# Moving the low-part subtraction of 32 weight pieces from VectorE to GpSimd, with a new order of work

## The chip, the cores and the metric

The program runs on one core of a Trainium2 chip. The metric is device time in microseconds (us): 932.86 us is the median of three runs (932.21 to 934.22). The engines have short names: PE (TensorE), DVE (VectorE), ACT (ScalarE), POOL (GpSimd) and SP (SyncE, which issues the loads here). A change of under 0.2% (1.9 us) can't be told from none with this kernel.

## What is computed

Two steps, all in fp32. Attention over 8 batches, 8 heads, 576 positions of 64 numbers, where each position sees only a few others (a band of 32 for four heads, every 32nd position for the other four); and a feed-forward layer on the 4608 tokens that come out:

```python
attn = softmax(mask(q @ k.T / 8)); x = (attn @ v)          # x: 4608 x 512
h  = x @ w_in                                              # 512 -> 2048
sp = np.maximum(h, 0.0) + np.log1p(np.exp(-np.abs(h)))
g  = h * erf(sp)
out = g @ w_out                                            # 2048 -> 512
```

The weights arrive as 64-bit floats.

## The kernel before

**Split numbers.** A product that is to be exact to fp32 is taken as three products of reduced precision. Each operand is split into a high part (a cast on ACT) and a low part (the number less its high part, on DVE). This is done for x (`xhi`, `xlo`), for g (`ghi`, `glo`) and for the weights (`pair[:, 0]`, `pair[:, 1]`).

**Weight pieces.** `weight()` prepares one of 32 pieces (pieces 0 to 15 of w_in, 16 to 31 of w_out), each 128x512. SP loads the 64-bit words; three DVE operations (`bits0`, `bits1`, `bits2`, L628 to L641) make an fp32 number in `w`; ACT casts it to the high part (L646); a fourth DVE operation, `split_lo_w` (L649), subtracts to get the low part.

**Attention units.** `heads()` does one batch and one pair of heads (called b0 hp3 for batch 0, pair 3): scores on PE (L400, masks L413), softmax on DVE and ACT (maximum L436, exponentials L457 or L472, sums, reciprocal L490 and L491), the multiplication by the reciprocal on POOL (L498, for most units), transposes on PE (L507) with a copy by ACT (L513), and the product with v on PE (L526), whose result is split into `xhi` and `xlo` (L545, L550). The eight units of batches 0 and 1 come first; later ones are strewn into the feed-forward work.

**Feature tiles.** `ftile()` handles 384 tokens and 128 of the 2048 features: 12 matmuls of the first product (L678, tile `h`), ten steps of activation on ACT (L686, L716) and DVE (L683, L713, L719) that end in `ghi` and `glo`, and 9 matmuls of the second product (L750, tiles `o`). There are 192 of these. `h` has three buffers, so a tile's first product waits until the `glo` of the tile three before it is done. "First product 5" below is that of the fifth tile.

**Order.** Nothing is scheduled by hand. Every operation has an engine, a duration by formula and a sort key; `Plan.order()` walks through time and lets each engine take the ready operation with the smallest key. The keys are the tables `FT`, `KW` and `KP`. The list that comes out is emitted in that order, so each engine runs its list strictly in order. Three rules of the planner matter below. `TWO` and `op.locks` make some DVE operations and every POOL operation exclude one another. `BLOCK = 254` counts PE's instructions, with a pause possible at each 254th while the next instructions are brought in. And `warm()` puts matmuls without use into PE's gaps.

Of the kernel before, what the change touches and what calls it, by code (L numbers as in the profile page):

```python
# [8 lines left out]
F32 = mybir.dt.float32  # L9
# [4 lines left out]
ALU = mybir.AluOpType  # L14
# [17 lines left out]
FT = (31.6335, -135.614, 224.291, 52.3709, -149.741, 22.9733, 45.4447, 151.185, -55.3448, 2.76331, -71.5147, 15.0393)  # L32
KI = 6.0
KW = (
# [39 lines left out]
PAIRS = (
# [192 lines left out]
def attention_moe(  # L267
# [52 lines left out]
    def act(n, fixed=0.093):  # L320
        return fixed + n / 1200.0
# [643 lines left out]
```

## Time and profile before

| | |
|---|---|
| median of 3 runs | 932.86 us |
| profiled execution | 933.05 us, span 931.3 us |
| PE busy | 909.7 us (98%) |
| DVE busy | 686.7 us (74%), 1352 instructions |
| ACT busy | 653.4 us (70%) |
| POOL busy | 60.9 us (7%), 59 instructions |
| mean granted PE clock | 0.993 of full |

An engine's busy share is a mean over a program with three parts: a head of some 60 us in which attention for the first two batches and the first weights are made ready, a long middle of feature tiles, and a short end. The table by stretches (below) is to be read before the totals. A row of the timeline gives start, duration, engine, line, operation, tiles, and in brackets how long the engine was idle before it and what ended that.

### The profile page before, as it was taken

What the parts mean: (1) busy time and instruction counts of PE and PEld (TensorE: products, weight loads), DVE (VectorE), ACT (ScalarE), POOL (GpSimd) and SP (SyncE); (2) the same over time, 40 slices, a digit from 0 to 9 for tenths busy, and PEclk for the clock granted to TensorE, in tenths of its full rate; (3) what the DMA queues carried; (4) which work ended last, traced back from release to release, by engine and by line L of the source; (5) the groups of instructions that cost most, each with busy time, mean ns of one, the idle gap of its engine ahead of it and who ended that gap; (6) DMA issues with size and microseconds to landing.
All of it is one profiled execution on the core that took longest, in us unless ns stands there. A gap on an engine that the chain in (4) does not pass through costs nothing.

```text
span 931.3 us, 20134 instructions
## 1 busy us (share of the span) xinstructions
PE 909.7 (98%) x8166; PEld 809.6 (87%) x8169; DVE 686.7 (74%) x1352; ACT 653.4 (70%) x1476; POOL 60.9 (7%) x59
## 2 busy tenths in 40 slices
PE   5789999999999999999999999999999999999998
PEld 4678888898888889988888899998898899999997
DVE  5999999996757766669886876667876666666664
ACT  5687887887776767667666666766766766766765
POOL 2200012110101100001110100000100000000000
PEclk9799999999999999999999999999999999999999
DMA  9994124321313010013312300002300200000000
GB/s 336 391 362 154 62 57 73 61 34 48 78 58 86 30 64 35 27 57 105 99 56 92 124 17 1 34 1 73 135 1 30 70 1 1 34 1 0 34 1 35
DMA packets 23421, 68.86 MB, mean 74 GB/s; under 512 B 2592, under 2 KB 3232, under 8 KB 23328
## 3 DMA queue, kind: packets, MB, share of 16 engines
q1 hardware_dynamic: 20736, 62.86, 18.9%
q0 software_dynamic: 2592, 4.72, 3.6%
q8 instruction: 64, 1.05, 0.5%
q14 instruction: 29, 0.24, 0.1%
HBM read 53.41 MB, written 14.16 MB: 73 GB/s over the span
## 4 chain that ended last, share of the span: by engine, by line
PE 90%; DVE 4%; ACT 3%; issue 1%; DMA 1%; SPq 0%; POOL 0%; ACTq 0%; POOLq 0%
PE h L678 41%; PE o L750 40%; PE s L400 3%; PE x L526 3%; PE t L507 2%; PE s L526 1%; DMA qk<-qk_loc 1%; ACT b L686 1%; DVE a L683 1%; DVE b L683 1%; ACT a L686 1%; PE s L507 1%; DVE glo L719 1%; ACT sm L472 0%; DVE h L713 0%
## 5 line engine op out<-in xcount | busy, mean ns | idle before, releaser
L750 PE MATMUL o<-pair,ghi 128*128 128x512 f32 x1152 | 361.4, 395 | 0.2 <-ACT ghi L716 0.2
L678 PE MATMUL h<-xhi,pair 128*128 128x384 f32 x1536 | 302.4, 339 | 0.6 <-DVE glo L719 0.6
L678 PEld LDWEIGHTS h<-xhi,pair 128*128 128x128 f32 x1536 | 271.4, 188 | 16.5 <-DVE glo L719 2.6
L686 ACT ACTIVATE b<-b 128x384 f32<-128x384 f32 x384 | 200.4, 522 | 77.2 <-DVE b L683 73.8
L750 PEld LDWEIGHTS o<-pair,ghi 128*128 128x128 f32 x1152 | 209.8, 188 | 32.4 <-ACT ghi L716 0.7
L750 PE MATMUL o<-pair,glo 128*128 128x512 f32 x576 | 224.8, 390 | 0.0
L683 DVE SCALAR_TENSOR_TENSOR a<-h,a 128x384 f32<-128x384 f32 x192 | 106.3, 553 | 83.3 <-ACT a L686 82.8
L678 PE MATMUL h<-xlo,pair 128*128 128x384 f32 x768 | 164.4, 336 | 0.0
L686 ACT ACTIVATE a<-h 128x384 f32<-128x384 f32 x192 | 93.5, 487 | 100.9 <-PE h L678 100.2
L683 DVE SCALAR_TENSOR_TENSOR a<-a,h 128x384 f32<-128x384 f32 x192 | 105.5, 549 | 68.9 <-ACT b L686 68.9
L713 DVE TENSOR_TENSOR h<-b,h 128x384 f32<-128x384 f32 x192 | 107.0, 557 | 46.2 <-ACT b L686 45.8
L678 PEld LDWEIGHTS h<-xlo,pair 128*128 128x128 f32 x768 | 136.0, 188 | 0.0
L750 PEld LDWEIGHTS o<-pair,glo 128*128 128x128 f32 x576 | 108.1, 188 | 23.7 <-DVE glo L719 0.3
L686 ACT ACTIVATE a<-a 128x384 f32<-128x384 f32 x192 | 100.3, 523 | 26.6 <-DVE a L683 26.1
L719 DVE TENSOR_TENSOR glo<-h,ghi 128x384 fp32r<-128x384 f32 x192 | 105.7, 550 | 11.7 <-ACT ghi L716 10.2
L716 ACT CAST ghi<-h 128x384 fp32r<-128x384 f32 x192 | 90.5, 471 | 29.1 <-DVE h L713 15.1
L683 DVE SCALAR_TENSOR_TENSOR b<-b,a 128x384 f32<-128x384 f32 x192 | 108.7, 566 | 1.0
L686 ACT ACTIVATE b<-a 128x384 f32<-128x384 f32 x192 | 101.0, 526 | 4.4
L498 POOL TENSOR_TENSOR sm<-sm,r 128x768 f32<-128x768 f32 (+3 forms) x36 | 45.0, 1249 | 435.3 <-DVE r L491 330.9
L436 DVE TENSOR_REDUCE mx<-s 128x12 f32<-128x768 f32 (+3 forms) x37 | 28.8, 784 | 10.6 <-PE s L413 10.3
L766 ACT COPY ob<-o 128x512 f32<-128x512 f32 x54 | 31.0, 588 | 2.7 <-PE o L750 2.2
L526 PEld LDWEIGHTS x<-pt,v 64*64 64x64 f32 x1392 | 24.4, 135 | 6.9 <-issue 4.4
(49 smaller groups left out, 511.4 us busy)
## 6 DMA issues: line engine op xcount, KB each, us to landing
out<-ob SPq DMA_DIRECT2D x36, 256.0 KB, 2.0
v<-v_loc SPq DMA_DIRECT2D x13, 640.0 KB, 4.1
words<-w_in SPq DMA_DIRECT2D x16, 512.0 KB, 8.6
words<-w_out SPq DMA_DIRECT2D x16, 512.0 KB, 9.1
qk<-qk_loc SPq DMA_DIRECT2D x13, 592.0 KB, 3.8
qk<-qk_str SPq DMA_DIRECT2D x12, 608.0 KB, 3.8
v<-v_str SPq DMA_DIRECT2D x16, 384.0 KB, 3.3
out<-ob POOLq DMA_DIRECT2D x18, 256.0 KB, 4.6
```

Of the source, the lines that this page charges most:

```text
L436: yield nc.vector.tensor_reduce(out=mx[:, parts[i], :units], in_=wide(of(s, i)), axis=mybir.AxisListType.X, op=ALU.max)
L498: yield (nc.gpsimd if pool_norm else nc.vector).tensor_tensor(out=d, in0=d, in1=spread(rc, i), op=ALU.mult)
L507: yield nc.tensor.transpose(bank(t, h)[:, 128 * w : 128 * w + 128], sm[:, h, c : c + 128], ident)
L526: yield nc.tensor.matmul(bank(px, m)[h * D : (h + 1) * D, a * n : (a + 1) * n], values(rows, (2 * a + h) * D), pt[rows, h, c : c + n], sta ...
L678: yield nc.tensor.matmul(ph[:, :CH], win[4 * s + cc][:, w, fs], x[cc][:, c0 : c0 + CH], start=(i == 0), stop=(i == len(terms) - 1))
L683: yield nc.vector.scalar_tensor_tensor(out=out, in0=in0, scalar=scalar, in1=in1, op0=op0, op1=op1)
L686: yield nc.scalar.activation(dst, src, func, bias=bias[i], scale=scale)
L713: yield nc.vector.tensor_tensor(out=ph[:, :CH], in0=bb.tile, in1=ph[:, :CH], op=ALU.mult)
L716: yield nc.scalar.copy(ghi.tile, ph[:, :CH])
L719: yield nc.vector.tensor_tensor(out=glo.tile, in0=ph[:, :CH], in1=ghi.tile.bitcast(F32), op=ALU.subtract)
L750: yield nc.tensor.matmul(po.tile, g[:, ts], wout[f][:, w], start=(f == first_f and i == 0), stop=(f == last_f and i == 2),)
L766: yield nc.scalar.copy(ob.tile, po.tile)
```

## The change

`split_lo_w` is issued on GpSimd for all 32 pieces. In the planner it gets another duration and the engine `pool`. The tables `FT`, `KW` and `KP` have new numbers throughout, so that the whole program stands in another order.

```diff
-FT = (31.6335, -135.614, 224.291, 52.3709, -149.741, 22.9733, 45.4447, 151.185, -55.3448, 2.76331, -71.5147, 15.0393)
+FT = (22.3696, -56.4987, 194.434, 53.4017, -119.353, -10.553, 57.033, 135.384, -40.4697, 20.41, -109.684, 14.539)
...
+POOL_LO = tuple(range(32))
...
         def split_lo_w():
-            yield nc.vector.tensor_tensor(out=pair[:, 1], in0=w.tile, in1=pair[:, 0].bitcast(F32), op=ALU.subtract)
+            yield (nc.gpsimd if i in POOL_LO else nc.vector).tensor_tensor(
+                out=pair[:, 1], in0=w.tile, in1=pair[:, 0].bitcast(F32), op=ALU.subtract
+            )
...
         op = add("act", act(n), key + 0.3, split_hi, [op], [pair], [w])
+        if i in POOL_LO:
+            return add("pool", 0.1 + n / 500.0, key + 0.4, split_lo_w, [op], [], [w, pair]), pair
         return add("dve", dve(n), key + 0.4, split_lo_w, [op], [], [w, pair]), pair
```

The lines after it move by one to five (L649 becomes L650, L678 becomes L683, L719 becomes L724, L750 becomes L755).

What moves is shown at three places. The first is DVE at its first weight piece (piece 2, `w_2`), before:

```order
L641 SCALAR_TENSOR_TENSOR w_2_190<-words_98,w_2_190 128x512
L481 TENSOR_REDUCE r_2_235<-sm_2_158 128x12
L490 TENSOR_SCALAR r_2_235<-r_2_235 128x12
L491 RECIPROCAL r_2_235<-r_2_235 128x12
L649 TENSOR_TENSOR pair_283<-w_2_190,pair_283 128x512
```

DVE at the same piece now:

```order
L642 SCALAR_TENSOR_TENSOR w_2_156<-words_94,w_2_156 128x512
L465 TENSOR_SCALAR mx_1_159<-mx_1_159 128x5
L437 TENSOR_REDUCE mx_2_253<-s_2_170 128x12
L491 TENSOR_SCALAR r_1_198<-r_1_198 128x5
L492 RECIPROCAL r_1_198<-r_1_198 128x5
```

The subtraction into `pair` is gone from DVE's list; it is the first thing in POOL's list now.

The second place is PE between the first products of tiles 4 and 5 (`h_1076` and `h_1182` before), after the last matmul of tile 4. `s_2_927` is the last attention unit of batch 1, `pair_846` and `pair_997` are weight pieces of w_out. Before:

```order
L507 MATMUL s_2_927<-ident,sm_2_928 128x128 x6
L750 MATMUL o_0_1110<-pair_846,ghi_1037 128x512 x2
L750 MATMUL o_0_1110<-pair_846,glo_1048 128x512
L750 MATMUL o_0_1120<-pair_846,ghi_1037 128x512 x2
L750 MATMUL o_0_1120<-pair_846,glo_1048 128x512
L526 MATMUL s_2_927<-qk_1_2_766,v_2_856 64x54 x22
L750 MATMUL o_0_1158<-pair_846,ghi_1037 128x512 x2
L750 MATMUL o_0_1158<-pair_846,glo_1048 128x512
L750 MATMUL o_0_1110<-pair_997,ghi_1124 128x512 x2
L750 MATMUL o_0_1110<-pair_997,glo_1153 128x512
L750 MATMUL o_0_1120<-pair_997,ghi_1124 128x512 x2
L750 MATMUL o_0_1120<-pair_997,glo_1153 128x512
```

PE in the same place now (`h_1046` and `h_1211` are tiles 4 and 5, `s_0_917` is the last attention unit of batch 1, `s_0_1164` the first of batch 2):

```order
L508 MATMUL s_0_917<-ident,sm_0_918 128x128 x6
L755 MATMUL o_0_1081<-pair_980,ghi_1006 128x512 x2
L755 MATMUL o_0_1081<-pair_980,glo_1036 128x512
L755 MATMUL o_0_1089<-pair_980,ghi_1006 128x512 x2
L755 MATMUL o_0_1089<-pair_980,glo_1036 128x512
L527 MATMUL s_0_917<-qk_1_0_638,v_0_744 64x32 x32
L527 MATMUL s_0_917<-qk_1_0_638,qk_1_0_639 64x32 x4
L755 MATMUL o_0_1144<-pair_980,ghi_1006 128x512 x2
L755 MATMUL o_0_1144<-pair_980,glo_1036 128x512
L401 MATMUL s_0_1164<-qk_0_1033 32x64 x40
L683 MATMUL h_1211<-xhi_76,pair_437 128x384
```

Six matmuls of the second product have gone behind first product 5, and the 40 score matmuls of the first unit of batch 2 have come ahead of it.

The third place is DVE between the `glo` of the first tile (`glo_1048`) and that of the second (`glo_1153`). Before, all that stands there:

```order
L683 SCALAR_TENSOR_TENSOR a_1006<-a_1006,h_962 128x384
L498 TENSOR_TENSOR sm_2_928<-sm_2_928,r_2_1018 128x768
L683 SCALAR_TENSOR_TENSOR b_1033<-b_1033,a_977 128x384
L550 TENSOR_TENSOR xlo_83<-s_1_3_858,xhi_79 128x18x18
L550 TENSOR_TENSOR xlo_83<-s_1_3_859,xhi_79 128x18x14
L683 SCALAR_TENSOR_TENSOR b_1043<-b_1043,a_1006 128x384
L641 SCALAR_TENSOR_TENSOR w_18_959<-words_673,w_18_959 128x512
L713 TENSOR_TENSOR h_898<-b_1033,h_898 128x384
L628 TENSOR_SCALAR w_7_1117<-words_690 128x512
L683 SCALAR_TENSOR_TENSOR a_1108<-h_1076,a_1108 128x384
L635 SCALAR_TENSOR_TENSOR w_7_1117<-words_690,w_7_1117 128x512
L719 TENSOR_TENSOR glo_1153<-h_898,ghi_1124 128x384
```

DVE between the first and second tile's `glo` now has 20 rows (two for a reciprocal, eight of 384 numbers, four of `xlo`, two `bits0`, four `bits1` or `bits2`); the last twelve are:

```order
L688 SCALAR_TENSOR_TENSOR b_1062<-b_1062,a_967 128x384
L642 SCALAR_TENSOR_TENSOR w_9_915<-words_702,w_9_915 128x512
L688 SCALAR_TENSOR_TENSOR a_1079<-h_1046,a_1079 128x384
L629 TENSOR_SCALAR w_19_1095<-words_645 128x512
L629 TENSOR_SCALAR w_20_1137<-words_751 128x512
L636 SCALAR_TENSOR_TENSOR w_19_1095<-words_645,w_19_1095 128x512
L636 SCALAR_TENSOR_TENSOR w_20_1137<-words_751,w_20_1137 128x512
L718 TENSOR_TENSOR h_854<-b_1039,h_854 128x384
L551 TENSOR_TENSOR xlo_80<-s_0_917,xhi_76 128x256
L551 TENSOR_TENSOR xlo_80<-s_0_917,xhi_76 128x320
L718 TENSOR_TENSOR h_885<-b_1062,h_885 128x384
L724 TENSOR_TENSOR glo_1206<-h_854,ghi_1157 128x384
```

Twelve rows have become twenty: two more pieces are begun here, and the last unit's `xlo` stands here as well.

## Rows read from the trace of the kernel before

**Rows 1.** The table by stretches of time: stretch, its length, then busy us (and instructions) of PE, PE's weight loads, DVE, ACT and POOL, the granted PE clock, the share of the DMA engines, GB/s.

```profile
20.00:30.00 10.00, 4.90 (x164) 3.45 (x155) 8.05 (x21) 7.58 (x37) 2.84 (x3) 0.91 1.02 371
30.00:40.00 10.00, 8.12 (x222) 6.54 (x223) 9.60 (x23) 7.10 (x29) 3.53 (x4) 0.67 1.03 403
...
50.00:60.00 10.00, 8.26 (x88) 5.71 (x87) 9.90 (x25) 8.38 (x36) 1.94 (x2) 1.00 1.03 409
60.00:70.00 10.00, 9.33 (x128) 8.17 (x126) 10.00 (x22) 7.58 (x18) 0.00 (x0) 1.00 0.81 297
...
100.00:120.00 20.00, 19.44 (x99) 17.45 (x98) 20.00 (x41) 15.73 (x35) 0.00 (x0) 1.00 0.20 73
...
900.00:931.30 31.30, 27.47 (x134) 23.69 (x132) 15.71 (x31) 18.01 (x39) 0.00 (x0) 1.00 0.07 26
```

**Rows 2.** The timeline of PE in the head, around three idle times that end with "issue".

```profile
22.21 0.44 PE L400 MATMUL s<-qk,qk 64*64 64x64 f32 x10 [1.92 <-issue]
...
24.67 0.88 PE L400 MATMUL s<-qk,qk 64*32 64x64 f32 x67
28.66 0.46 PE L400 MATMUL s<-qk,qk 64*32 64x64 f32 x13 [3.12 <-issue]
...
32.38 0.55 PE L526 MATMUL s<-pt,v 64*64 64x32 f32 x24
34.68 1.47 PE L526 MATMUL s<-pt,v 64*64 64x32 f32 x48 [1.75 <-issue]
```

**Rows 3.** The timeline of PE further on: first product 1, the first useless matmul of the wait for the softmax of b1 hp3, the second half of that unit's product with v, and first product 4.

```profile
43.69 2.37 PE L678 MATMUL h<-xhi,pair 128*128 128x384 f32 x8
...
54.74 0.38 PE L863 MATMUL warm<-con 128*128 128x512 bf16 x1
...
60.74 0.90 PE L526 MATMUL s<-qk,v 64*64 64x54 f32 x42 [0.67 <-ACT qk L513]
61.57 1.68 PE L678 MATMUL h<-xhi,pair 128*128 128x384 f32 x8
```

**Rows 4.** The timeline of ACT for the same softmax: its first and last exponential, and the last copy of its transposes.

```profile
52.24 0.31 ACT L472 ACTIVATE sm<-s,mx 128x64 f32<-128x64 f32 x1
...
55.80 0.39 ACT L472 ACTIVATE sm<-s,mx 128x64 f32<-128x64 f32 x1
...
60.10 0.59 ACT L513 COPY qk<-s 128x384 f32<-128x384 f32 x1
```

**Rows 5.** Groups of instructions by line and shape: count, busy us in all, mean ns of one, idle time before them.

```profile
L649 DVE TENSOR_TENSOR pair<-w,pair 128x512 fp32r<-128x512 f32 x32 | 22.8, 712 | 0.9 <-ACT pair L646 0.9
...
L498 POOL TENSOR_TENSOR sm<-sm,r 128x768 f32<-128x768 f32 x13 | 19.4, 1493 | 90.7 <-DVE r L491 51.8 <-ACT b L686 22.0 <-PE o L750 8.3
...
L448 DVE TENSOR_TENSOR sm<-s,mx 128x640 f32<-128x640 f32 x13 | 10.6, 818 | 0.3
```

**Rows 6.** The timeline of POOL: two of its twelve multiplications in the first 60 us.

```profile
20.11 0.72 POOL L498 TENSOR_TENSOR sm<-sm,r 128x320 f32<-128x320 f32 x1 [2.89 <-DVE r L491]
...
38.14 1.26 POOL L498 TENSOR_TENSOR sm<-sm,r 128x640 f32<-128x640 f32 x1 [0.44 <-ACT qk L513]
```

**Rows 7.** The timeline of DVE: the four operations beside POOL's work that took longer than their like (20.19, 30.62, 34.06 and 38.19), and at 32.90 the like of the second.

```profile
20.19 1.20 DVE L641 SCALAR_TENSOR_TENSOR w<-words,w 128x512 uint32<-128x512 uint32 x1
...
30.62 0.72 DVE L464 TENSOR_SCALAR mx<-mx 128x5 f32<-128x5 f32 x1
...
32.90 0.16 DVE L464 TENSOR_SCALAR mx<-mx 128x5 f32<-128x5 f32 x1
...
34.06 1.26 DVE L628 TENSOR_SCALAR w<-words 128x512 uint32<-128x512 uint32 x2
...
38.19 1.75 DVE L649 TENSOR_TENSOR pair<-w,pair 128x512 fp32r<-128x512 f32 x1
```

**Rows 8.** The timeline of DVE without a gap; from one start to the next is what an operation costs DVE.

```profile
64.19 0.68 DVE L641 SCALAR_TENSOR_TENSOR w<-words,w 128x512 uint32<-128x512 uint32 x1
64.79 0.55 DVE L713 TENSOR_TENSOR h<-b,h 128x384 f32<-128x384 f32 x1
65.25 0.42 DVE L628 TENSOR_SCALAR w<-words 128x512 uint32<-128x512 uint32 x1
65.59 0.55 DVE L683 SCALAR_TENSOR_TENSOR a<-h,a 128x384 f32<-128x384 f32 x1
...
67.12 0.68 DVE L649 TENSOR_TENSOR pair<-w,pair 128x512 fp32r<-128x512 f32 x1
67.72 0.55 DVE L713 TENSOR_TENSOR h<-b,h 128x384 f32<-128x384 f32 x1
```

**Rows 9.** The timeline of PE later: first products 5, 8 and 11.

```profile
68.95 1.38 PE L678 MATMUL h<-xhi,pair 128*128 128x384 f32 x7
...
80.06 1.66 PE L678 MATMUL h<-xhi,pair 128*128 128x384 f32 x8
...
93.73 1.55 PE L678 MATMUL h<-xhi,pair 128*128 128x384 f32 x8
```

**Rows 10.** The timeline of DVE: the `glo` of tile 1, and those of tiles 5 and 8, for which first products 8 and 11 wait.

```profile
60.72 0.55 DVE L719 TENSOR_TENSOR glo<-h,ghi 128x384 fp32r<-128x384 f32 x1
...
79.46 0.55 DVE L719 TENSOR_TENSOR glo<-h,ghi 128x384 fp32r<-128x384 f32 x1
...
91.49 0.55 DVE L719 TENSOR_TENSOR glo<-h,ghi 128x384 fp32r<-128x384 f32 x1
```

More of the change, by code (lines that the diff above doesn't have):

```diff
@@ new lines @@
+    (5.66987, 13.0282, 55.8745, 38.2764, -15.9681, -36.756, 33.4004),
+    (-18.7339, -39.1163, 76.4337, -28.9027, 10.2532, 24.2041, 30.6549),
+    (-15.4896, -11.984, 39.6104, 19.5357, -7.74296, -11.7955, -40.5758),
+    (17.5401, 38.2042, 121.253, 14.5964, -41.3024, -43.7492, 21.1018),
+    (72.5436, -2.47781, 1.95628, -12.642, 62.4187, 30.7351, -3.2493),
+    (32.9714, 14.3441, -41.7302, 3.07189, 9.0242, 46.2111, 15.2472),
+    (54.623, 23.7062, 30.603, 5.95764, 9.0606, 31.5463, 37.9128),
+    (99.1807, 117.579, 14.7102, 0.856988, 42.0313, 44.0342, -13.5854),
@@ new lines @@
+    (181.976, 87.2448, 162.43, 24.3666, 131.02, 72.183, 127.636),
+    (97.9926, 232.179, 138.727, 162.708, 197.927, 116.499, 223.073),
+    (149.582, 217.989, 179.504, 261.135, 173.959, 152.093, 233.931),
+    (139.299, 113.299, 244.924, 260.874, 227.01, 256.022, 261.547),
+    (245.847, 201.102, 202.904, 219.678, 257.7, 216.473, 220.811),
+    (219.04, 236.591, 269.74, 244.921, 260.22, 258.551, 288.033),
+    (227.079, 272.329, 241.105, 272.617, 252.119, 274.64, -79.8311),
+    (242.583, -71.686, 253.986, 255.399, 260.846, 286.519, -57.5012),
@@ new lines @@
+    (299.89, 7.0902, 388.18, 367.844, 327.156, 50.8514, -1.66736),
+    (368.909, 41.1273, 404.906, 25.5317, 65.8247, -2.42926, 34.1271),
+    (333.532, 11.6209, -23.6141, 30, 16.8656, 28.0746, -24.5951),
+    (-21.8889, 66.3196, 79.6323, -19.6143, 58.2492, 20.6542, 29.5598),
+    (-16.9561, -81.56, -73.3898, -43.1701, 25.5148, -17.3561, -63.4817),
+    (-47.8575, 52.7288, -45.2402, 48.9679, -37.6956, -9.91878, -38.4614),
+    (-46.4028, -30.6651, -22.7336, -15.072, -15.952, -19.3536, -22.7128),
@@ new lines @@
+    (20.367, 11.7704, 32.4, 6.23905, -8.11303, -16.7471, -29.3541),
+    (41.7767, 39.5077, -31.3991, 40.4667, 84.8511, -32.1912, -31.5126),
+    (25.9401, 20.0181, 47.8103, 33.4559, -23.371, 5.11266, 3.10776),
+    (69.3454, 28.2065, 63.2799, 45.3715, 30.2949, 39.8847, 22.9595),
+    (46.2723, -1.63389, 55.8803, 55.0971, 7.58647, 31.6189, -10.4984),
+    (-39.3636, 37.8553, -20.752, -17.8468, -20.5648, -43.9449, 10.4532),
+    (-59.8325, -2.50562, -56.1516, -55.004, -42.9456, -52.8569, -52.8667),
@@ L73 @@
+    (-27.4153, -13.8723, -32.8034, -47.3267, -44.4922, -28.105, -34.4584),
+    (-68.8922, -69.0877, -72.5331, -73.1939, -25.1887, -23.8768, -78.0878),
 )
```

32 lines of the change are left out of this document (removed), and 8 rows, old and new, of the table KW.

## The prediction

> **What bounds the kernel now.** I read the table by stretches first. From 70 us on PE is busy without a break: the largest idle time in a stretch is 0.56 us (19.44 busy of 20, 100 to 120), and the end costs 3.83 (27.47 of 31.30) [rows 1]. PE's useful work is the same after the change: the same matmuls, fewer `warm` ones. So the time is set by when PE gets into its unbroken run and by whether DVE lets it stay there. Before that run PE has gaps: busy 4.90 of 10 in 20 to 30, 8.12 in 30 to 40 at a granted clock of 0.67, 8.26 in 50 to 60 [rows 1].
>
> The timeline of PE tells of two kinds. Three idle times end with "issue", of 1.92, 3.12 and 1.75 us; PE waited for no engine. They lie inside blocks of small matmuls, and PE goes on at 22.21, 28.66 and 34.68, 6.45 and 6.02 us apart [rows 2]. Counted in the order with the planner's 254, each is at a point where new instructions are brought in. The other kind is the softmax of b1 hp3: PE fills from 54.74 with useless matmuls, and only goes on with the unit's second product half at 60.74 and first product 4 at 61.57 [rows 3]; ACT ran its exponentials from 52.24 to 56.19 and its last copy at 60.10 [rows 4], and the `glo` of tile 1, for which first product 4 waits too, ended at 61.27 [rows 10].
>
> Then DVE. It is busy 9.90 of 10 in 50 to 60, and 10.00 and 20.00 of the whole in 60 to 70 and 100 to 120 [rows 1]. First product 8 starts at 80.06, right behind the `glo` of tile 5 (79.46 + 0.55); first product 11 starts at 93.73, 1.7 behind the `glo` of tile 8 [rows 9, 10]. PE and DVE are in step here: what DVE loses past that, PE loses.
>
> **What it removes and adds.** 32 subtractions leave DVE. They were busy 22.8 us [rows 5], but from one start to the next cost 0.60 (67.12 to 67.72) [rows 8]: 32 x 0.60 = 19.2 us of DVE, of which nine (5.4) stood ahead of the first `glo`. POOL gets 32 operations of 128x512. No such one is in the trace. From 320 numbers in 0.72 and 640 in 1.26 [rows 6] a number costs 1.69 ns, so 512 cost 0.72 + 192 x 0.00169 = 1.04 us. Below it can't be than the 0.72 of 320; above, by the mean of 768 (1.49) [rows 5]. I take 1.05: 34 us on an engine with 870 idle. Most are needed long after; the first four are needed for first product 1.
>
> The hidden price is DVE itself. Beside POOL's multiplications four DVE operations are too long [rows 7]: 1.20 for a `bits2` that otherwise takes 0.68 (0.52 more; it ran on until POOL's 0.72 from 20.11 was over [rows 6] and then for its own time), 0.72 for a small operation of 0.16 (0.56), 1.26 for two `bits0` of 0.42 each (0.42), 1.75 for a subtraction of 0.68 (1.07, beside POOL's 1.26 from 38.14). That is 2.57 us over the twelve POOL operations of the head: 0.21 each. Bounds per subtraction: 0, and 1.07, the longest seen. I take 0.22, by the mean of the twelve; so each subtraction that moves gives DVE 0.60 - 0.22 = 0.38.
>
> The Trainium skill speaks against such a change: "Perfetto Trace Analysis", section "Optimizing Scalar/DVE Operations", says that VectorE and GpSimd share an SBUF read port, so that moving work between the two may not help; and "SBUF — State Buffer", section "Who interferes with whom", says that the loser is fully blocked for the whole instruction. Rows 7 agree on the blocking; how often it strikes here they show for the head alone. By the page taken at its worst, every subtraction blocks DVE for its full length and the change loses; that is the second rival.
>
> **Step 1, up to 34.7 us: 0.** Counted with the same 254, PE's third, fourth and fifth refill fall in the scores of b0 hp3, the scores of b1 hp1 and the product with v of b0 hp0, as before. From one refill to the next PE needs 3 to 4.5 us of work and 6.0 to 6.5 of waiting in all [rows 2], so the freed DVE time is hidden behind "issue" here. The load for b0 hp0 moved forward on SP's queue gains nothing either, for the same reason. If the stalls moved, this term would be within 0.5 of zero either way.
>
> **Step 2, to first product 4: -3.3.** From the fifth refill on, the new order has less to do before first product 1: the refill falls at 0.8 of the product with v of b0 hp0, not at 0.3, which is some 0.7 us, and DVE no longer has two weights' operations ahead of b1 hp1's reciprocal. I put first product 1 at 42.4 for 43.69 [rows 3]: -1.3. The scores of b1 hp3 then follow at once; before, the 1.5 us product with v of b1 hp0 stood between. That makes -2.8. DVE has the maximum of that unit close behind, and ACT starts its exponentials at 48.1 for 52.24 and ends at 52.2 for 56.19 [rows 4]. PE has a product with v, two first products and a block of scores to do meanwhile, about 6.6 us. On ACT stand behind the exponentials five operations, then the two copies of this unit with one more between them (0.5 to 0.6 each): 56.0 for 60.69. Then come one exponential, the cast and the `glo` of tile 1: 58.25 for 61.27, and first product 4 at 58.3 for 61.57: **-3.3**. Each estimate comes from durations of single rows, and they add up to an uncertainty of some 1.5.
>
> **Step 3, first product 5: +2.0 back.** Before, from first product 4 to 5 PE needed 68.95 - 61.57 = 7.38 [rows 3, 9]. Now six matmuls of the second product are fewer (six of 0.23, -1.4), 80 score passes more (+1.05, by 0.88 for 67 of them [rows 2]) and the product with v has 72 and not 44 passes (+0.55): 7.6, so PE would be there at 65.9. But it needs the `glo` of tile 2, and DVE has more to do for it than before: from `glo` 1 to `glo` 2 stood twelve operations, now twenty. With the steps of rows 8 (0.47 for 384 numbers, 0.34 for `bits0`, 0.60 for `bits1` and `bits2`) and 1.5 for the four `xlo` and 0.3 for the reciprocal: 8 x 0.47 + 4 x 0.60 + 2 x 0.34 + 1.5 + 0.3 = 8.6. One subtraction runs on POOL beside it (0.22), and a cast is some 0.2 late. `glo` 2 is done at 58.25 + 9.0 = 67.3, and PE waits 1.4. Compared by work done (six matmuls less, 1.4; scores 1.05 more, so 0.35 behind), PE's lead shrinks from 3.3 to 68.95 - 67.3 - 0.35 = 1.3: **+2.0**.
>
> **Step 4, tiles 5 to 11: 0.** DVE from `glo` 2 to `glo` 8 has 28 operations of 384 numbers, 10 `bits1` or `bits2`, 4 `bits0`, four softmax operations of 640 (0.82 at most [rows 5]) and a reciprocal: 13.2 + 6.0 + 1.4 + 3.3 + 0.3 = 24.2, plus seven POOL operations at 0.22: 25.7. `glo` 8 ends at 93.0. PE took 93.73 - 68.95 = 24.78 from first product 5 to 11 [rows 9], 1.0 of it scores; now it has six more matmuls (1.4) and six transposes (0.8) in place of the scores, 26.0, and would start first product 11 at 93.3. So DVE is 0.3 ahead, with no reserve to speak of, as before. After that the subtractions that DVE no longer does add up in its favour; of the 0.56 that PE idled in 100 to 120 little is to be had.
>
> **Sum.** 0 - 3.3 + 2.0 + 0 = -1.3 on the profiled execution's 933.05: 931.75. That execution (span 931.3 and 1.75 around it) is 0.19 above the median, so against it: 932.86 - 1.3 = **931.6**. Own range of this case 929.9 to 933.3, from DVE's loss per operation between 0 and 0.5 and the 1.5 of step 2.
>
> **Rival A: the lead of step 2 is kept.** DVE has `glo` 2 before PE comes for it. For it: DVE's list up to the first `glo` lacks 5.4 us, so `glo` 1 may come before 58.25 and all behind it too. Also the clock: granted 0.67 in 30 to 40 [rows 1] after the idle times of rows 2, and it could rise sooner. Against: `glo` 1 waits for ACT's copies and not for DVE in step 2. Time: 932.86 - 3.3 = 929.6.
>
> **Rival B: slower by the shared block.** Place: first product 11 and the tiles behind it, where PE and DVE are in step. From 0.60 per subtraction on DVE has gained nothing. At 0.85, midway between that and 1.07: `glo` 8 comes seven times 0.63 = 4.4 later than in step 4, at 97.4 for PE's 93.3: 4.1 lost, less the lead of 1.3. What DVE saves later against what it still loses is worth some 1 more or less. Time 932.86 + 2.8 = 935.7. For it: here DVE's list is full of `bits` operations, the kind that was blocked. Against: only four of twelve were hit.
>
> **Rival C: POOL's queue delays the softmax.** Five subtractions stand directly ahead of a multiplication of the softmax in POOL's list (pieces 2, 3, 0, 4 and 6), which runs in strict order, and behind the multiplication is the transpose on PE. If a subtraction takes 1.5 and not 1.05, that is 0.45 at each, and with three of the five on the path +1.3 against the forecast: 932.9. For it: the idle time of 0.67 before 60.74 shows that such a chain is not hidden [rows 3]. Against: in ACT's list the exponentials that the multiplication needs stand, four times of five, behind the cast that the subtraction needs, so it has 1.5 us and more before the multiplication can start.
>
> **How the numbers follow.** Forecast 0.50, A 0.26, B 0.16, C 0.08. Faster by over 0.2% (1.87, so under 931.0): all of A, and 0.16 of the forecast's 0.50: 0.42. Slower by over 0.2%: B and 0.02 of C and of the forecast each: 0.20. Within: 0.38. The range 928.4 to 936.0 takes in A with 1.2 beyond it and B, and leaves out some 0.1 at either end.
>
> **What would show it.** Step 1: idle times that end with "issue" near 22, 28 and 34. Step 2: first product 4 near 58, and useless matmuls no longer from 54.74 to 60. Step 3: PE idle for 1 to 2 us before first product 5, released by the `glo` of DVE. Step 4: first product 11 at about 93, and subtractions of 1.0 to 1.1 on POOL with DVE operations a third of the time longer beside them. It would be wrong if the stalls with "issue" went, if first product 5 waited for nothing, or if DVE's `bits` took over 1.2 on average from 70 us on.

## The result, and the profile after the change

The changed kernel took 940.64 us (median of 6 runs, 938.75 to 943.35), the kernel before on the same chip 932.93 (6 runs): a ratio of 1.0082, 95% interval 1.0066 to 1.0099. It is slower by 0.8%; the forecast of 931.6 and its range up to 936.0 both missed. The profiled execution is the slowest of the six, 943.35 with a span of 941.6 us, so its places lie up to 2.7 us behind the median.

Start with the page's totals (engine, busy us, share of the span, number of instructions).

```profile
PE 914.9 (97%) x8159; PEld 811.2 (86%) x8163; DVE 686.8 (73%) x1320; ACT 654.1 (69%) x1476; POOL 104.8 (11%) x91
```

DVE has 32 instructions less than before, and they were busy 22.8 us [rows 5]. Yet DVE is busy as long as before (686.7 on that page): what left it came back as longer operations. The groups by line and shape say which. Columns: count, busy us in all, mean ns, then the idle time before them.

```profile
L650 POOL TENSOR_TENSOR pair<-w,pair 128x512 fp32r<-128x512 f32 x32 | 44.6, 1396 | 100.2 <-ACT pair L647 93.7 <-issue 6.6
L636 DVE SCALAR_TENSOR_TENSOR w<-words,w 128x512 uint32<-128x512 uint32 x32 | 26.3, 824 | 0.1
L642 DVE SCALAR_TENSOR_TENSOR w<-words,w 128x512 uint32<-128x512 uint32 x32 | 24.9, 778 | 0.0
...
L629 DVE TENSOR_SCALAR w<-words 128x512 uint32<-128x512 uint32 x32 | 16.1, 510 | 9.1 <-DMA words<-w_in 8.9 <-POOL pair L650 0.2
...
L688 DVE SCALAR_TENSOR_TENSOR b<-b,a 128x384 f32<-128x384 f32 x192 | 116.5, 607 | 1.1
```

`bits1` (L636) and `bits2` (L642) had means of 679 and 695 ns before, `bits0` (L629) 434; `b<-b,a`, a step of the activation, had 566 and was busy 108.7 us, 7.8 less than now. A subtraction takes POOL 1.40. A mean hides that a few operations are much longer and the rest unchanged; the timelines show it. POOL first (start, us), then DVE, which stands in the same stretch without a gap.

```profile
92.20 1.29 POOL L650 TENSOR_TENSOR pair<-w,pair 128x512 fp32r<-128x512 f32 x1 [3.20 <-ACT pair L647]
...
103.75 1.29 POOL L650 TENSOR_TENSOR pair<-w,pair 128x512 fp32r<-128x512 f32 x1 [3.98 <-ACT pair L647]
106.32 1.28 POOL L650 TENSOR_TENSOR pair<-w,pair 128x512 fp32r<-128x512 f32 x1 [1.28 <-ACT pair L647]
```

```profile
91.86 0.55 DVE L688 SCALAR_TENSOR_TENSOR a<-h,a 128x384 f32<-128x384 f32 x1
92.32 1.58 DVE L688 SCALAR_TENSOR_TENSOR b<-b,a 128x384 f32<-128x384 f32 x1
93.83 0.55 DVE L724 TENSOR_TENSOR glo<-h,ghi 128x384 fp32r<-128x384 f32 x1
...
103.80 1.79 DVE L642 SCALAR_TENSOR_TENSOR w<-words,w 128x512 uint32<-128x512 uint32 x1
105.51 0.54 DVE L688 SCALAR_TENSOR_TENSOR a<-a,h 128x384 f32<-128x384 f32 x1
105.98 0.55 DVE L724 TENSOR_TENSOR glo<-h,ghi 128x384 fp32r<-128x384 f32 x1
106.44 1.58 DVE L688 SCALAR_TENSOR_TENSOR b<-b,a 128x384 f32<-128x384 f32 x1
```

The operation at 92.32 starts 0.12 after POOL's subtraction, which ends at 93.49, and itself ends at 93.90: it stood until POOL was nearly done, and ended 0.41 behind it. It cost 1.03 more than its like (0.55), and the `glo` behind it, for which PE waits, came that much later. On PE:

```profile
62.51 1.66 PE L683 MATMUL h<-xhi,pair 128*128 128x384 f32 x8 [0.79 <-DVE glo L724]
...
71.41 1.66 PE L683 MATMUL h<-xhi,pair 128*128 128x384 f32 x8
...
94.43 1.66 PE L683 MATMUL h<-xhi,pair 128*128 128x384 f32 x8 [0.97 <-DVE glo L724]
...
98.66 1.55 PE L683 MATMUL h<-xhi,pair 128*128 128x384 f32 x8
...
106.57 1.66 PE L683 MATMUL h<-xhi,pair 128*128 128x384 f32 x8 [0.86 <-DVE glo L724]
```

These are first products 4, 5, 10, 11 and 13. The wait at 94.43 is for the `glo` of 93.83, the one at 106.57 for that of 105.98, behind the `bits2` of 1.79 at 103.80. Between 60 and 200 us PE waits 3.7 us for `glo` in all, and 2.4 for ACT's copies of `o` into `ob`, for which it waited nowhere there before; ACT in turn waits 16.5 us for `b<-b,a` (2.9 before). By stretches (length, then busy time and count of PE, weight loads, DVE, ACT, POOL, then the granted clock; [rows 1]):

```profile
20.00:30.00 10.00, 6.45 (x197) 5.09 (x193) 8.20 (x21) 9.22 (x48) 4.92 (x5) 0.67 0.87 295
30.00:40.00 10.00, 7.55 (x143) 5.94 (x144) 9.02 (x18) 6.87 (x30) 5.21 (x6) 0.67 1.00 387
...
50.00:60.00 10.00, 9.95 (x213) 8.02 (x212) 9.89 (x23) 8.99 (x37) 3.10 (x4) 1.00 1.02 397
...
100.00:120.00 20.00, 18.76 (x169) 16.22 (x168) 19.25 (x34) 14.53 (x31) 4.67 (x4) 1.00 0.15 50
```

PE is idle for 1.24 us in 100 to 120, where it was 0.56; in each of the other stretches of 20 us from 80 to 200 it is idle for 0.5 to 1.1, where it was 0.1 at most. Against the kernel before, first product 4 is 0.9 us late, number 5 2.5, number 11 4.9, number 21 8.7 and number 30 9.7 (187.78 for 178.11); the span is 10.3 longer. Since the orders differ, the same first product doesn't stand for the same work done; against the run f1 below, which has the changed kernel's order, the lag is 2.0 at number 5, 9.8 at number 30 and 10.1 at number 60 and at the last. So all but some 2 us of it is lost between first products 5 and 30.

### The profile page after: what moved, and what is told of

Same layout as the page of the kernel before. It is cut to its first block, busy times and chain, and to the rows that moved or that the text cites. A ratio compares the mean times of both kernels' runs of the same rounds, so it can differ in the third digit from the quotient of the medians.

```text
span 941.6 us, 20153 instructions
## 1 busy us (share of the span) xinstructions
PE 914.9 (97%) x8159; PEld 811.2 (86%) x8163; DVE 686.8 (73%) x1320; ACT 654.1 (69%) x1476; POOL 104.8 (11%) x91
## 3 DMA queue, kind: packets, MB, share of 16 engines
q8 instruction: 64, 1.05, 0.5%
## 4 chain that ended last, share of the span: by engine, by line
PE 80%; DVE 9%; DMA 4%; ACT 3%; issue 3%; POOL 0%; SPq 0%; POOLq 0%; DVEq 0%; ACTq 0%
PE h L683 36%; PE o L755 36%; PE x L527 3%; PE s L401 3%; DVE a L688 2%; DVE b L688 2%; PE t L508 2%; ACT b L691 2%; DMA qk<-qk_str 1%; DMA words<-w_in 1%; DVE w L636 1%; DMA words<-w_out 1%; DVE glo L724 1%; DVE h L718 1%; DVE w L642 1%
## 5 line engine op out<-in xcount | busy, mean ns | idle before, releaser
L755 PE MATMUL o<-pair,ghi 128*128 128x512 f32 x1152 | 361.3, 395 | 2.7 <-ACT ob L771 2.4
L683 PE MATMUL h<-xhi,pair 128*128 128x384 f32 x1536 | 303.0, 339 | 3.9 <-DVE glo L724 3.7
L683 PEld LDWEIGHTS h<-xhi,pair 128*128 128x128 f32 x1536 | 270.8, 188 | 21.0 <-DVE glo L724 7.7
L755 PEld LDWEIGHTS o<-pair,ghi 128*128 128x128 f32 x1152 | 210.0, 188 | 36.3 <-ACT ob L771 4.1
L755 PE MATMUL o<-pair,glo 128*128 128x512 f32 x576 | 224.8, 390 | 0.0
L683 PE MATMUL h<-xlo,pair 128*128 128x384 f32 x768 | 164.4, 336 | 0.0
L683 PEld LDWEIGHTS h<-xlo,pair 128*128 128x128 f32 x768 | 136.0, 188 | 0.0
L755 PEld LDWEIGHTS o<-pair,glo 128*128 128x128 f32 x576 | 108.1, 188 | 23.7 <-DVE glo L724 0.3
L688 DVE SCALAR_TENSOR_TENSOR b<-b,a 128x384 f32<-128x384 f32 x192 | 116.5, 607 | 1.1
L724 DVE TENSOR_TENSOR glo<-h,ghi 128x384 fp32r<-128x384 f32 x192 | 105.6, 550 | 15.7 <-ACT ghi L721 15.0
L650 POOL TENSOR_TENSOR pair<-w,pair 128x512 fp32r<-128x512 f32 x32 | 44.6, 1396 | 100.2 <-ACT pair L647 93.7
L401 PEld LDWEIGHTS s<-qk 64*32 64x32 f32 (+1 forms) x1616 | 21.3, 117 | 10.6 <-issue 4.5
```

Of the source, the lines that this page charges most:

```text
L401: yield nc.tensor.matmul(bank(s, h)[m * j : m * (j + 1), 64 * t : 64 * (t + 1)], queries(rows, q0, m), keys_of(rows, q0), start=(h, j) not ...
L650: yield (nc.gpsimd if i in POOL_LO else nc.vector).tensor_tensor(out=pair[:, 1], in0=w.tile, in1=pair[:, 0].bitcast(F32), op=ALU.subtract)
L683: yield nc.tensor.matmul(ph[:, :CH], win[4 * s + cc][:, w, fs], x[cc][:, c0 : c0 + CH], start=(i == 0), stop=(i == len(terms) - 1))
L688: yield nc.vector.scalar_tensor_tensor(out=out, in0=in0, scalar=scalar, in1=in1, op0=op0, op1=op1)
L724: yield nc.vector.tensor_tensor(out=glo.tile, in0=ph[:, :CH], in1=ghi.tile.bitcast(F32), op=ALU.subtract)
L755: yield nc.tensor.matmul(po.tile, g[:, ts], wout[f][:, w], start=(f == first_f and i == 0), stop=(f == last_f and i == 2),)
```

## The experiments

Two theories stood at the start. Theory 1: while POOL subtracts, DVE is held up, for about as long as the subtraction cost DVE itself; the relief for which the order was made does not come. Theory 2: the new order is the worse one whatever engine subtracts (loads moved, a lower clock in the head). Throughout, DVE's loss beside POOL's work on the pieces is worked out from the timelines up to 230 us: each DVE operation's time less that of its like, where it is 0.06 or more. Some expectations quote it counted from 0.25 up, which gives 4.9 and 8.8 for what the table below has as 5.2 and 9.6.

**Order and engine apart.** Two kernels keep one and undo the other, two mix them.

```diff
# e1, in the changed kernel (e3 and e4: DVE, or POOL, for pieces 2, 3, 0, 4, 1, 18, 6, 17, 16 alone)
-            yield (nc.gpsimd if i in POOL_LO else nc.vector).tensor_tensor(
+            yield (nc.gpsimd if i in () else nc.vector).tensor_tensor(
# e2, in the kernel before
-            yield nc.vector.tensor_tensor(out=pair[:, 1], in0=w.tile, ...
+            yield nc.gpsimd.tensor_tensor(out=pair[:, 1], in0=w.tile, ...
```

> The changed kernel's order, with all 32 subtractions issued on DVE again at the places where they stand in that order. Theory 1 (lock): a subtraction on POOL holds DVE up, by about 0.55 us each by the longer operations of the changed kernel's trace, at spots where PE waits for a glo; without it the time goes back to 933 to 936, though DVE has 32 x 0.60 = 19 us more of its own. Theory 2 (order): the order sought anew is the worse one, whatever engine subtracts; 939 to 943. If the order needs POOL's help after all, DVE's 19 us more show as waits for glo and the time goes over 943.

> The kernel before with its own order; only the engine of the 32 subtractions changes, each stays where it was among the other instructions. Theory 1 (lock): 936 to 940, with DVE operations beside POOL's subtractions longer by about 0.55 us per subtraction. Theory 2 (order): 931 to 933.5, since the engine alone does no harm and DVE has a little more room.

> The changed kernel's order; the first nine subtractions (all ahead of first product 5) on DVE, the other 23 on POOL. If the loss of the head comes from POOL's queue (the softmax's multiplication waits behind a subtraction) and from blocked DVE operations there, first product 5 comes 2 us or more earlier than in the changed kernel (71.4) and the time is 936 to 938.5. If the order makes the head late, first product 5 stays at 71 or later and the time at 940 or above.

> The changed kernel's order; the first nine subtractions on POOL, the other 23 on DVE. If the blocks of DVE behind 70 us cost the 7 us by which the changed kernel falls back from first product 5 to the end, the time is 934 to 937. If DVE's own 0.60 per subtraction costs the same as the blocking, 939 to 942. If POOL did help there, over 942.

Beside 932.99 for the kernel before: e1 941.72 (ratio 1.0095, interval 1.0080 to 1.0110), e2 941.91 (1.0096, 1.0081 to 1.0111), e3 942.79 (1.0102, 1.0086 to 1.0119), e4 941.86 (1.0093, 1.0073 to 1.0113). Either edit alone costs what both cost together, so the two prices don't add. In the new order it makes no difference clear of noise which engine subtracts: POOL's help is worth nothing there. But theory 1's number for e1 (933 to 936) fell, and theory 2's for e2 (931 to 933.5) as well; e2 lies above theory 1's 936 to 940 too. e3 gains nothing with the head's nine on DVE (first product 5 at 70.94), so the loss isn't made in the head; e4 came out where DVE's own 0.60 costs as much as the hold. e1's waits from 70 to 200 us show a DVE that is late by its own load, with no operation held by a subtraction:

```profile
PE h L683 <- DVE glo L724: 4.3, 8, 0.9
```

So the order does need a lighter DVE. What was missing was a run in which it has one.

**The relief without the hold.** POOL writes zeros in place of the subtraction (f1 in the new order, f4 in the old), or copies one operand, so that the high part stands in the low part's place (f2). f3 follows another trace, see below.

```diff
# f1, f4 (f2: nc.gpsimd.tensor_copy(pair[:, 1], pair[:, 0].bitcast(F32)))
-            yield (nc.gpsimd if i in POOL_LO else nc.vector).tensor_tensor(...)
+            yield nc.gpsimd.memset(pair[:, 1].bitcast(F32), 0.0)
# f3, in e2
-            yield nc.gpsimd.tensor_tensor(out=pair[:, 1], ...
+            yield (nc.vector if i in (13, 14) else nc.gpsimd).tensor_tensor(out=pair[:, 1], ...
```

> The changed kernel's order; in place of each subtraction POOL fills the low part with zeros (the low part of the weights is left out of the result). POOL writes and reads nothing, DVE has 32 subtractions less. Theory 1 (POOL's subtraction costs DVE as much as it saves, because the two hold each other up while both read; the order was made for a DVE with less to do): with that gone the order is as good as planned, DVE's operations have their short times, the time is 925 to 931. Theory 2 (the new order is worse in itself, by its loads, its head and the clock there): 936 to 940, with waits before first products 6 to 21 as in the changed kernel.

> The changed kernel's order; in place of each subtraction POOL copies the high part into the low part (one operand read in place of two; the low part of the weights is left out of the result). If reading one operand is enough to hold DVE up for the whole of POOL's operation, DVE's long operations stay and the time is 937 to 942. If it needs two operands or mixes freely, the time is that of the run with the zeros, within 1.

> The old order with 30 subtractions on POOL; only pieces 13 and 14, whose subtractions stand ahead of a copy-out of ob in POOL's queue and wait there for ACT, are on DVE. In the run with all 32 on POOL the copies out went 2 to 4 us later, DVE waited 2.4 us for the buffer at 163.9 and PE 3.1 at 166.5. If that queue is the cause, first product 26 lags 1.3 to 3 instead of 6, first product 27 2 to 3 instead of 7.6, and the time is 934 to 937. If the blocking of DVE is the cause of all of the 9, it stays at 940 to 942.

> The old order; POOL fills the low part with zeros in place of all 32 subtractions (the low part of the weights is left out of the result). What 32 subtractions less on DVE are worth in the old order when nothing is held up: first product 12 at 98.9 or before, time 930.5 to 932.5 since only waits of 0.6 us in all lie between 70 and 200 and the head does not wait for DVE. If DVE's load had been the bound of the head, 927 to 930.

Beside 932.58: f1 932.62 (0.9997, 0.9982 to 1.0011), f2 932.39 (0.9996, 0.9980 to 1.0012), f3 937.43 (1.0045, 1.0031 to 1.0059), f4 932.11 (0.9996, 0.9984 to 1.0008). The new order with a relieved DVE is as fast as the old kernel, 8 us better than with the subtraction; that settles it against theory 2. A fill differs from the subtraction in more than the hold: it waits for no cast and leaves `w` free sooner. But the copy in f2 waits for the cast as the subtraction does and is no slower, DVE waited only 0.2 us for POOL to free `w` in the changed kernel (the `bits0` row above), and the granted clock of f1's profiled execution isn't higher than that of the kernel before (0.991 for 0.993). It is not better: f1's 925 to 931 fell too. Nor does the old order gain from 32 subtractions less (f4 is 0.5 below by the medians, and anywhere from 1.5 below to 0.7 above by its interval). So even free, the relief was worth nothing measurable. In f1's trace PE is without a gap where it had waited:

```profile
80.00:100.00 20.00, 20.00 (x106) 18.18 (x104) 19.09 (x40) 17.05 (x38) 3.55 (x5) 1.00 0.18 67
100.00:120.00 20.00, 20.00 (x177) 17.96 (x177) 18.88 (x38) 17.26 (x37) 2.29 (x4) 1.00 0.25 89
```

and its groups have their short means again:

```profile
L636 DVE SCALAR_TENSOR_TENSOR w<-words,w 128x512 uint32<-128x512 uint32 x32 | 22.7, 713 | 0.1
L642 DVE SCALAR_TENSOR_TENSOR w<-words,w 128x512 uint32<-128x512 uint32 x32 | 21.8, 681 | 0.0
...
L650 POOL MEMSET pair<- 128x512 f32 x32 | 18.3, 574 | 97.8 <-DVE w L642 85.8 <-issue 6.9 <-PE o L753 5.1
```

**What e2 lost beside it: POOL's queue.** In the old order with POOL, first product 21 is only 1.3 us late, number 27 7.6. The timeline of POOL in e2 over that stretch:

```profile
150.83 1.30 POOL L649 TENSOR_TENSOR pair<-w,pair 128x512 fp32r<-128x512 f32 x1 [6.39 <-ACT pair L646]
154.17 1.66 POOL L649 TENSOR_TENSOR pair<-w,pair 128x512 fp32r<-128x512 f32 x1 [2.05 <-ACT pair L646]
155.77 1.85 POOL L772 DMA_DIRECT2D out<-ob  x2
159.80 1.29 POOL L649 TENSOR_TENSOR pair<-w,pair 128x512 fp32r<-128x512 f32 x1 [2.18 <-ACT pair L646]
161.03 0.86 POOL L772 DMA_DIRECT2D out<-ob  x1
```

The third copy out was issued at 157.45 in the kernel before, here at 161.03: it stands behind the subtraction of piece 13, which waits for ACT. The weight tile `w` and the output tile `ob` share their buffers, so DVE's `bits0` waits for that transfer, and PE for the `glo` behind it. DVE, then PE:

```profile
163.89 0.76 DVE L628 TENSOR_SCALAR w<-words 128x512 uint32<-128x512 uint32 x2 [2.39 <-DMA out<-ob]
```

```profile
166.50 1.86 PE L678 MATMUL h<-xhi,pair 128*128 128x384 f32 x8 [3.09 <-DVE glo L719]
```

f3 takes pieces 13 and 14 alone out of that queue. In its trace the copies out go in time and first product 27 is 0.7 us late:

```profile
151.96 0.87 POOL L772 DMA_DIRECT2D out<-ob  x1 [1.75 <-ACT ob L766]
154.41 0.86 POOL L772 DMA_DIRECT2D out<-ob  x1 [1.58 <-ACT ob L766]
158.15 0.91 POOL L772 DMA_DIRECT2D out<-ob  x1 [2.88 <-ACT ob L766]
```

About half of e2's loss (8.9 to 4.9 us) was the queue behind those two subtractions (f3 is 0.4 above the range expected for that); most of the other half goes when the subtractions become fills (f4).

**What the hold depends on, and where it costs.** Three fills in place of a subtraction are longer than it and only write; two copies are as long and read one operand (f2 and g4 serve for their times alone). g2 takes the hold away in one stretch; g3 is the only candidate for a faster kernel that the traces suggested.

```diff
# g1: the fill three times; g4: the copy twice; g2, in the changed kernel:
+            if i in (9, 19, 20, 7, 5, 22, 21, 23, 10, 11, 8, 26):
+                yield nc.gpsimd.memset(pair[:, 1].bitcast(F32), 0.0)
+            else:
+                yield nc.gpsimd.tensor_tensor(out=pair[:, 1], ...
# g3, in the kernel before
-            yield nc.vector.tensor_tensor(out=pair[:, 1], ...
+            yield (nc.gpsimd if i in (2, 3, 0, 4, 1, 6, 16, 19, 17) else nc.vector).tensor_tensor(...
```

> The changed kernel's order; POOL fills each low part with zeros three times over (low parts left out of the result), some 1.6 us of POOL for each piece, longer than the subtraction's 1.40. POOL only writes. If what holds DVE up is that POOL reads from SBUF while it works, nothing comes of the length: DVE's long operations beside it stay at one or two, and the time is 931.5 to 934. If it is the length of POOL's work whatever it does, the time is 939 to 943, as with the subtractions.

> The changed kernel's order; POOL copies the high part into the low part twice (low parts left out of the result): 1.58 us for each piece, one operand read. If reading one operand is enough, and the length of it counts, DVE loses 10 us or more up to 220 us (4.9 with one copy, 19.4 with the subtraction) and the time is 935 to 941. If two operands have to be read, DVE loses no more than some 5 us and the time stays at 932 to 934.

> The changed kernel; only the twelve subtractions between first product 5 and first product 20 (67 to 128 us) are replaced by a fill with zeros (the low part of those twelve pieces is left out of the result), the nine ahead and the eleven behind stay subtractions on POOL. If the loss is made where PE and DVE are in step, between first products 5 and 21, that lag is 2 to 3 us in place of 7.7 and the time is 933.5 to 936.5. If every subtraction takes its share wherever it stands, 12 of 32 give back 3: 937 to 938.5.

> The old order with only the nine subtractions ahead of first product 5 on POOL, the other 23 on DVE. In the run with 30 on POOL first product 4 came 1.0 us earlier than in the kernel before. If DVE's relief in the head is worth that and nothing is lost behind it, 931 to 932.5, which would beat both kernels by little; if the blocks there eat it, 932.5 to 934.

Beside 932.52: g1 932.06 (0.9992, 0.9979 to 1.0005), g4 933.99 (1.0020, 1.0009 to 1.0032), g2 936.70 (1.0049, 1.0031 to 1.0066), g3 933.46 (1.0009, 0.9998 to 1.0021). g1 decides between reading and length: 1.66 us of writing for each piece does no harm to the time. Yet a fill isn't without a hold: 12 operations of DVE met one, where one or two were expected. Two fills of g1, and DVE beside them:

```profile
165.58 0.53 POOL L652 MEMSET pair<- 128x512 f32 x1
...
183.19 0.53 POOL L652 MEMSET pair<- 128x512 f32 x1
```

```profile
165.67 0.68 DVE L636 SCALAR_TENSOR_TENSOR w<-words,w 128x512 uint32<-128x512 uint32 x1
...
183.28 0.72 DVE L629 TENSOR_SCALAR w<-words 128x512 uint32<-128x512 uint32 x1
```

Both operations begin 0.09 after POOL's. `bits1`, with two tiles to read, takes its usual 0.68; `bits0`, with one, takes 0.72 for its 0.42.

One copy is enough to hold what the subtraction holds. POOL, then DVE in f2:

```profile
103.40 0.62 POOL L650 CAST pair<-pair 128x512 fp32r<-128x512 f32 x1 [1.26 <-ACT pair L647]
```

```profile
103.53 0.88 DVE L686 SCALAR_TENSOR_TENSOR b<-b,a 128x384 f32<-128x384 f32 x1
```

So f2's and g4's times, on the branch where two operands have to be read, misled: a copy does hold DVE, but for 0.3 to 0.4 each; g4's loss lies between its two expectations. g2 lies between its two expectations, 0.2 above the first: twelve of 32 subtractions give back 3.5 of the 7.7 us by the medians; that those twelve cost more than their share of 2.9 is not clear of noise. In its trace the lag grows by 1.7 from first product 5 to 21 (by 6.2 in the changed kernel), and by 1.0 more up to 30, where subtractions stand again. g3 gains nothing; 931 to 932.5 fell.

**One long instruction or several short ones.** The copies differ from the subtraction in two things, operands and length of one instruction. Splitting the subtraction changes the second alone.

```diff
# h1 (h2: four parts), in the changed kernel
-            yield (nc.gpsimd if i in POOL_LO else nc.vector).tensor_tensor(...)
+            for c in range(0, n, n // 2):
+                cs = slice(c, c + n // 2)
+                yield nc.gpsimd.tensor_tensor(out=pair[:, 1, cs], in0=w.tile[:, cs], ...
```

> The changed kernel with each subtraction on POOL as two instructions of 256 columns. Hold by instruction: a DVE operation that meets POOL's waits for the end of the one instruction in progress, so it waits half as long (0.4 in place of 0.84), and POOL's next half waits in turn. Then DVE loses some 10 us up to 220 us in place of 19.4 (as with two copies, 8.8), and the time is 934 to 937. Hold by the number of operands or by all of POOL's busy time: DVE loses 17 us or more and the time stays at 939 to 943.

> The changed kernel with each subtraction on POOL as four instructions of 128 columns. Hold by instruction: each wait is 0.2 to 0.3; DVE loses 5 to 10 us up to 220 us, the time is 932.5 to 936, unless POOL's own fixed cost per instruction makes the low parts late. Hold by all of POOL's busy time: DVE loses 19 us or more, time 939 or above.

Beside 932.16: h1 936.67 (1.0046, 1.0031 to 1.0061), h2 936.63 (1.0041, 1.0026 to 1.0055). The timelines of h1, POOL then DVE, show a hold that ends with the first half:

```profile
89.48 1.75 POOL L652 TENSOR_TENSOR pair<-w,pair 128x256 fp32r<-128x256 f32 x2 [3.20 <-ACT pair L647]
```

```profile
89.59 1.04 DVE L688 SCALAR_TENSOR_TENSOR b<-b,a 128x384 f32<-128x384 f32 x1
90.56 0.54 DVE L724 TENSOR_TENSOR glo<-h,ghi 128x384 fp32r<-128x384 f32 x1
```

It is 0.49 longer than its like, not 1.03, and POOL's two halves take 1.75 together, where the pair at 79.64 takes 1.43; that the second half waits for DVE in turn fits this. h1 came within its expectation for a hold by instruction; h2's loss did (7.4), its time is 0.6 above. All runs in the new order, by what stands for a piece's subtraction:

| in its place | us a piece | DVE's loss, us (operations held) | time less that of before, us |
|---|---|---|---|
| subtraction on DVE (e1) | - | 0 (DVE subtracts itself: 32 x 0.60) | +8.7 |
| subtraction on POOL (the change) | 1.40 | 19.4 (23) | +7.7 |
| two halves (h1) | 1.72 | 12.4 (30) | +4.5 |
| four quarters (h2) | 2.13 | 7.4 (34) | +4.5 |
| two copies (g4) | 1.46 | 9.6 (27) | +1.5 |
| one copy (f2) | 0.79 | 5.2 (15) | -0.2 |
| three fills (g1) | 1.66 | 3.9 (12) | -0.5 |
| one fill (f1) | 0.57 | 0.9 (2) | 0.0 |

Halves and copies show that the hold lasts for one instruction of POOL. The sixteen traces give its length as well. Of the `b<-b,a` that began from 62 to 230 us within an instruction of POOL on a piece, with over 0.2 us of it left, all 55 within a subtraction (or a part of one) and 15 of 16 within a copy (in the other, POOL's copy was the long one) were longer than their like, each by what POOL's instruction had left less 0.13 to 0.15; `bits0` within a fill was so too, 12 of 13. In the rows above: 93.49 - 92.32 = 1.17 left for 1.03, 104.02 - 103.53 = 0.49 for 0.33, 183.72 - 183.28 = 0.44 for 0.30. So a second operand adds nothing to a hit; length and the number of hits make the loss.

Quarters hold DVE less than halves and are no faster. In h2's trace PE waits for no low part; POOL's queue is in the way again, as in e2. POOL, ACT and PE:

```profile
154.22 2.18 POOL L652 TENSOR_TENSOR pair<-w,pair 128x128 fp32r<-128x128 f32 x4 [4.91 <-ACT pair L647]
156.34 1.84 POOL L777 DMA_DIRECT2D out<-ob  x2
```

```profile
161.53 0.59 ACT L771 COPY ob<-o 128x512 f32<-128x512 f32 x1 [1.35 <-DMA out<-ob]
```

```profile
162.17 0.73 PE L755 MATMUL o<-pair,ghi 128*128 128x512 f32 x2 [0.98 <-ACT ob L771]
```

Two copies out stand behind four quarters, ACT waits for the transfer to free its buffer, and PE for ACT. No run takes this away, so that it is all of the difference isn't shown. A version that beats the kernel before was not found.

## Why the prediction was wrong

**The term that failed is the hidden price of DVE.** The prediction took 0.22 us per subtraction, "by the mean of the twelve" multiplications of the head. Measured: 19.4 us over 32, so 0.61, with 23 of 32 hitting something and 0.84 per hit. Against the 0.60 saved, DVE's net is -0.01 in place of +0.38. The bounds held it (0 to 1.07), the choice within them was wrong for a reason that rows 7 already showed: only operations of the weight pieces and of the softmax's small numbers were held, and where the subtractions went, DVE runs the weight pieces and `b<-b,a` back to back. Beside the head's other eight multiplications DVE was in a reduction or on a PSUM tile (the tiles that PE writes lie in PSUM, the others in SBUF), or it had begun first, and then POOL's operation was the long one (1.00 at 13.46 for 320 numbers that else take 0.72). No operation with an operand in PSUM was held: of `a<-h,a`, `a<-a,h`, `h<-b,h` and `glo<-h,ghi`, 112 began from 62 to 230 us within a subtraction with over 0.2 us left, in the sixteen traces. The kernel's own text names most of the exposed operations: `TWO`, the list of what excludes POOL, has `bits0` to `bits2` and `n6`, which is `b<-b,a`. The sampled stretch was not the one to which the work moved. f1 prices the term: the same order without it is 7.7 us better, of the 9.0 between forecast (-1.3) and result (+7.7). POOL's 1.05 was 1.29 undisturbed, 1.40 on average; that alone was of no account on an engine with some 840 us idle.

The Trainium skill had the rule for this. "SBUF — State Buffer", section "Who interferes with whom", says that a VectorE instruction with two SBUF inputs contends with a GpSimd instruction that reads SBUF, and not with one that only writes it. The traces agree on both halves: 19.4 us of loss beside the subtractions, and none of the 17 `b<-b,a`, `bits1` and `bits2` that began within a fill with over 0.2 us left was held. The prediction quoted from that section only that the loser is fully blocked, and left out which operations are exposed.

**Step 1 (0)** failed in the profiled execution: first product 1 came at 47.35, not 42.4, with idle times for "issue" at 30.55 (4.10) and 38.68 (1.84) and not near 22, 28 and 34. PE waited 2.44 us before 16.98 for POOL's multiplications, ahead of which stood the subtraction of piece 2 (13.08 to 14.35). That resembles rival C, but POOL was idle before both and waited for DVE's reciprocals; the first was late because its small operation, 0.16 elsewhere, was held by that subtraction. DVE, then POOL:

```profile
13.47 0.90 DVE L491 TENSOR_SCALAR r<-r 128x5 f32<-128x5 f32 x1
```

```profile
14.68 0.72 POOL L499 TENSOR_TENSOR sm<-sm,r 128x320 f32<-128x320 f32 x1 [0.33 <-DVE r L492]
```

So it is the same term, at a place that step 1 put at nothing. It did not set the end: by first product 4 the lag was down to 0.9 us, and e3, with the head's nine on DVE, is no faster.

**Step 2 (-3.3)**: first product 4 was forecast at 58.3 and came at 62.51. Kernels with the same order but little hold have it at 58.43 (g4), 58.53 (g1), 60.54 (f1) and 60.67 (f2). e4 and g2, whose head is the changed kernel's, have it at 61.17 and 60.28. So the sum can be reached, but the head scatters by 2 us between profiled executions of like kernels (that of the changed kernel is its slowest run), and even a reached lead is given back later.

**Step 3** was right in its size and its engine, and not in its place: from first product 4 to 5 it forecast 9.0, with 1.4 of waiting for `glo` 2; measured are 71.41 - 62.51 = 8.90, with 1.35 of waiting ahead of the scores. DVE, then PE:

```profile
69.53 0.82 DVE L551 TENSOR_TENSOR xlo<-s,xhi 128x256 fp32r<-128x256 f32 x2 [0.19 <-ACT xhi L546]
...
70.73 0.55 DVE L724 TENSOR_TENSOR glo<-h,ghi 128x384 fp32r<-128x384 f32 x1
```

```profile
70.45 1.03 PE L401 MATMUL s<-qk 64*32 64x64 f32 x80 [1.35 <-issue]
```

The profile puts this wait down to "issue", but in all eleven traces of the new order PE goes on 0.10 us after DVE's last `xlo` of that unit, which reads the scores' tile. First product 5 then starts 0.13 behind the end of `glo` 2, with no wait of its own: the sign that the prediction named didn't show, though DVE's list was the bound.

**Step 4 (0)** is where the missed term struck. From first product 5 to 11 it forecast 26.0; f1, without the hold, took 25.56, the changed kernel 27.25. The larger error is the sentence behind it, that later subtractions "add up in its favour": from first product 11 to 30 the kernel before took 84.38, f1 82.95, the changed kernel 89.12, 4.7 us lost.

**Rival B** named the mechanism and the place, at 0.16. Its price was short: it put DVE's loss at 0.85 per subtraction and got +2.8, because it counted seven subtractions up to first product 11 and "some 1 more or less" behind. At 0.61 the measured price is +7.7. It treated the order as one with slack, while the order was made with the subtractions on POOL, and DVE lighter by 19 us: without that relief PE meets a late `glo` again and again up to first product 30, as e1 shows with no subtraction on POOL (+8.7). **Rival A** did not come: g1 and g4 had its lead at first product 4, and ended 0.5 below and 1.5 above the kernel before. **Rival C** did not come: ahead of each of its five multiplications POOL stood idle, for 0.33 to 4.97 us.

## What to carry to other kernels

In these runs VectorE paid for work on GpSimd that reads SBUF: price it by what stands beside it at the new place, with what is left of the one GpSimd instruction in progress per hit, and not by a mean over a place where VectorE does other things. An order made for a relief is a bet on it: here it is worse by 8 to 9 us than the old one when the relief fails, and no better when it comes, so first find what the relief is worth by taking the work away altogether (a fill in its place). In-order queues count too: a waiting subtraction ahead of a copy-out on GpSimd's queue cost 4 us through the buffer that the transfer held.

## What the hardware showed that was not expected

A fill on GpSimd, three times over and 1.66 us a piece, held DVE for only 3.9 us in all, while the two-operand subtraction of 1.40 held it for 19.4. Operations with one SBUF tile and a constant were held as well (`bits0` at 0.42 us for 512 numbers: four of them, 3.0 us in the changed kernel's trace, one of the four beside a multiplication), and from 62 us on they were the only ones that a fill held; so were operations of five numbers: one `mx<-mx` of 0.16 takes 0.72 already in rows 7.
